# Probabilities as the moving operand: the value product of windowed attention in column tiles, with DVE transposes in place of DMA transposes

## The chip, the cores and the metric

The kernel runs on one core of a Trainium2 chip. The metric is the device time of one execution in microseconds. Names of engines: PE is the tensor engine (PEld its weight loads), ACT the scalar engine, DVE the vector engine, POOL the GpSimd engine, SP the queue that issues DMAs.

## The reference

The output is `g * attention(x) + (1 - g) * swiglu(x)` over 2048 rows of 512 numbers. What matters here is the attention: 32 heads of 16 dimensions, and each query sees only the 256 keys that end at itself.

```python
H = 32; Dh = D // H; W = 256
qkv = (x @ wqkv).reshape(B, S, 3, H, Dh)...
scores = einsum("bhqd,bhkd->bhqk", q, k) * Dh ** -0.5
mask = (idx[:, None] - idx[None, :] >= 0) & (idx[:, None] - idx[None, :] < W)
p = softmax(where(mask, scores, -1e9))
o = einsum("bhqk,bhkd->bhqd", p, v)
a = o.transpose(...).reshape(B, S, D) @ wo
```

The other half, `silu(x @ w1) * (x @ w3) @ w2`, is most of the arithmetic, and its matmuls fill the time between the attention's steps.

## The kernel before

Heads are handled eight at a time (`c`), queries in pairs of 128-row tiles (`p`). A *score burst* makes scores, keys in the partitions, for the eight heads: four matmuls (or eight) in four row tiles of the array at once (strips of 32 of its rows, each with operands of its own). One ACT instruction takes the exponential of all of it, 128x2048, out of a single buffer `big` of four banks of PSUM, the memory that matmuls write to. POOL zeroes what the mask forbids.

```python
# score burst, exponential
big = ps.tile([P, 4, 512], F32, name="big")          # one buffer
for u in range(4):
    nc.tensor.matmul(big[:, u, k * 256:k * 256 + 2 * w],
                     lhsT=kt[32 * u:32 * u + 32, kb * P:(kb + 1) * P],
                     rhs=qz[32 * u:32 * u + 32, :, q0:q0 + w], start=True, stop=True)
nc.scalar.activation(out=e[:, :, 0:2 * n], in_=tl["big"][:, :, 0:2 * n], func=ACT.Exp, scale=SCALE)
```

A *value block* multiplies probabilities by V. The kernel before makes the 128x128 probabilities the stationary operand, so that 17 columns (16 of V and a column of ones, which sums the denominator) stream past it. The result has queries in the partitions; DVE divides it by the denominator, and a DMA turns it into the layout that the output projection needs.

```python
for h8 in range(8):
    ...                                              # two or three key blocks
    nc.tensor.matmul(pva[:, k, h8, :], lhsT=lhsT,    # lhsT: 128x128 probabilities
                     rhs=Vaug[:, kp, 8 * c + h8, :], # 17 columns
                     start=(bi == 0), stop=(bi == len(blocks) - 1))
...
nc.vector.reciprocal(out=st["rden"][:], in_=st["pva"][:, :, :, DH:DH + 1])
nc.vector.tensor_tensor(out=ocur[:], in0=st["pva"][:, :, :, 0:DH],
                        in1=st["rden"][:].to_broadcast([P, 2, 8, DH]), op=ALU.mult)
...
nc.sync.dma_start_transpose(out=OT[:, o:o + P], in_=...ocur...)
```

All instructions are put in order beforehand by a list scheduler in the kernel's own Python text. It knows a duration for each step, slots for the buffers (four PSUM banks `g` for everything but scores), and a due time for each burst (one every 2.55 us). The order on each engine is fixed by it; the hardware only waits.

Names in the lines below: `kt` keys, `qz` masked copies of the queries, `edm` and `ef` probabilities (key blocks on the diagonal and those further back), `tt`, `h` and `hT` the steps of the other half, `OT` the attention's output turned, `ot` a piece of the result. Lines shown are picked out of a view; "..." marks a cut within a sequence in time.

The softmax here doesn't subtract the row's maximum and nothing guards it: scores larger than these inputs give would overflow.

## Time and profile before

| | before |
|---|---|
| median of the first four runs | 257.91 us (257.75 to 258.07) |
| PE / ACT / DVE / POOL busy | 98 / 76 / 59 / 59 % |
| score bursts | 92, one every 2.57 us |
| value blocks | 28 of 48 matmuls, 4 of 24 |

The first lines are from the page of the profile: busy time, share and instructions of each engine, and then the chain of work that ended last, by engine and by line.

```profile
PE 250.7 (98%) x2755; PEld 124.1 (48%) x2755; DVE 151.0 (59%) x267; ACT 195.0 (76%) x143; POOL 150.0 (59%) x251
PE 94%; DMA 2%; SPq 1%; DVE 1%; issue 0%; DVEq 0%
PE g L361 32%; PE g L414 15%; PE g L556 14%; PE big L493 12%; PE g L255 11%; PE g L301 6%; PE g L443 5%; DMA wq_sb<-in_A_wqkv_dram 2%; DMA out_dram<-ot 1%; SPq L571 1%; DVE ot L450 0%; PE g L213 0%; SPq L106 0%; DVE Vaug L311 0%; SPq L453 0%
```

PE is busy 98% of the span and is 94% of the chain, so what shortens PE's work shortens the kernel, until something else becomes the chain. Line 556 is the value matmul and has 14% of the chain. A busy PE alone would not prove this, as the ends of matmuls are modelled in the trace; the chain does.

The next lines are groups of instructions by form: line, engine, operation, operands, count, then busy us and the mean ns of one, then idle time before them and who ended it.

```profile
L501 ACT ACTIVATE edm<-big 128x2048 bf16<-128x2048 f32 x60 | 112.6, 1877 | 29.1 <-PE big L493 16.3 <-POOL edm L510 8.0 <-POOL ef L515 4.6
L556 PE MATMUL g<-Vaug,edm 128*128 128x17 bf16 x992 | 41.5, 171 | 0.0
L562 DVE RECIPROCAL rden<-g 128x16 f32<-128x16 f32 x32 | 8.1, 255 | 12.6 <-PE g L556 12.3
L564 DVE TENSOR_TENSOR ocur<-g,rden 128x256 bf16<-128x256 f32 x32 | 13.6, 425 | 1.1
L510 POOL TENSOR_SCALAR_AFFINE_SELECT edm<-edm 128x512 bf16<-128x512 bf16 x128 | 78.6, 637 | 55.8 <-ACT edm L501 54.3
```

The exponential takes 1.88 us. The value matmuls' 171 ns each are latencies and overlap; their real rate is seen in the chain in order of time (start, us, what):

```profile
102.82 0.33 PE big L493 x8
103.15 0.97 PE g L361 x4
104.12 1.20 PE g L556 x48
105.32 0.23 PE g L361
```

A block of 48 value matmuls takes 1.20 us, 25 ns for each pair of weight load and matmul, and a score burst takes 0.33 us. The matmuls of 512 columns (line 361) take 0.216 us each: 1.73 us for eight. Four of them take 0.97 us where they follow a burst, 0.1 us more than their 0.86: I take this for the change of array mode at the burst, and call it a drain below. The old value block pays none: the matmul after it takes 0.23 us.

The last lines, from the timeline of instructions, show the loop through the single score buffer:

```profile
100.16 0.39 PE L493 MATMUL big<-qz,kt 32*128 32x512 bf16 x4
...
100.67 1.88 ACT L501 ACTIVATE edm<-big 128x2048 bf16<-128x2048 f32 x1 [0.72 <-POOL edm L510]
...
102.75 0.40 PE L493 MATMUL big<-qz,kt 32*128 32x256 bf16 x8
...
103.35 1.87 ACT L501 ACTIVATE ef<-big 128x2048 bf16<-128x2048 f32 x1
```

The exponential starts 0.51 us after this burst begins and ends at 102.55. The next burst begins 0.20 us later, and its exponential after another 0.60 us, one tanh being between. Over all bursts I measured 0.45 us from burst to exponential for bursts of eight matmuls and 0.51 for bursts of four, and from exponential to next burst at least 0.07 us. A turn of this loop thus costs at least about 2.38 us after a burst of eight matmuls and 2.44 after one of four. PE had 2.57 us of work for each turn: the loop was hidden, but only just.

### The profile page before, as it was taken

How to read it: one execution, taken by the hardware profiler on the slowest of the kernel's cores; microseconds unless marked ns; L12 is line 12 of the kernel's file. 1: busy time of each engine (PE TensorE's matmuls, PEld its weight loads, DVE VectorE, ACT ScalarE, POOL GpSimd, SP SyncE). 2: the span in 40 equal slices, each digit the busy share in tenths (PEclk: the TensorE clock that was granted, in tenths of full speed). 3: DMA queues.
4: the chain of work that ended last, by engine and by line, in shares of the span. 5: the costliest groups of instructions: out<-in, count | busy, mean ns of one | idle time of the engine just before them, and what ended most of it. 6: DMA issues, size and time to landing. Idle time of an engine off the chain costs nothing.

```text
span 256.1 us, 6562 instructions
## 1 busy us (share of the span) xinstructions
PE 250.7 (98%) x2755; PEld 124.1 (48%) x2755; DVE 151.0 (59%) x267; ACT 195.0 (76%) x143; POOL 150.0 (59%) x251
## 2 busy tenths in 40 slices
PE   7999999999999999999999999999999999999994
PEld 3545554555545445454555455544563555445552
DVE  2766758766576378456557465637465666454453
ACT  4788788778878888787979797888787878786700
POOL 4275757575565575754755757546737565566610
PEclk9999999999999999999999999999999999999999
DMA  6999921000000000000000000000001111101112
GB/s 196 349 227 286 230 67 13 13 10 8 9 21 3 10 13 11 13 0 13 12 13 14 11 8 5 14 10 13 12 13 13 51 49 47 50 13 50 32 32 87
DMA packets 27014, 13.05 MB, mean 51 GB/s; under 512 B 18309, under 2 KB 26981, under 8 KB 26985
## 3 DMA queue, kind: packets, MB, share of 16 engines
q1 hardware_dynamic: 26424, 12.51, 19.7%
q8 instruction: 21, 0.34, 0.5%
q10 hardware_dynamic: 528, 0.13, 0.2%
q14 instruction: 9, 0.07, 0.1%
q0 software_dynamic: 32, 0.00, 0.0%
HBM read 7.38 MB, written 2.11 MB: 37 GB/s over the span
## 4 chain that ended last, share of the span: by engine, by line
PE 94%; DMA 2%; SPq 1%; DVE 1%; issue 0%; DVEq 0%
PE g L361 32%; PE g L414 15%; PE g L556 14%; PE big L493 12%; PE g L255 11%; PE g L301 6%; PE g L443 5%; DMA wq_sb<-in_A_wqkv_dram 2%; DMA out_dram<-ot 1%; SPq L571 1%; DVE ot L450 0%; PE g L213 0%; SPq L106 0%; DVE Vaug L311 0%; SPq L453 0%
## 5 line engine op out<-in xcount | busy, mean ns | idle before, releaser
L501 ACT ACTIVATE edm<-big 128x2048 bf16<-128x2048 f32 x64 | 116.7, 1824 | 30.4 <-PE big L493 17.5
L510 POOL TENSOR_SCALAR_AFFINE_SELECT edm<-edm 128x512 bf16<-128x512 bf16 x128 | 78.6, 637 | 55.8 <-ACT edm L501 54.3
L515 POOL TENSOR_SCALAR_AFFINE_SELECT ef<-ef 128x512 bf16<-128x512 bf16 x112 | 67.6, 635 | 37.7 <-ACT ef L501 37.7
L361 PE MATMUL g<-xT,w_sb 128*128 128x512 bf16 (+2 forms) x352 | 89.0, 381 | 0.2 <-DVE Vaug L311 0.2
L501 ACT ACTIVATE ef<-big 128x2048 bf16<-128x2048 f32 x28 | 52.5, 1877 | 12.1 <-PE big L493 6.3
L361 PEld LDWEIGHTS <-w_sb 128*128 128x128 bf16 (+2 forms) x352 | 31.4, 100 | 38.2 <-issue 9.0
L378 DVE SCALAR_TENSOR_TENSOR h<-tt,g 128x512 bf16<-128x512 bf16 x40 | 27.4, 686 | 34.5 <-ACT tt L373 34.3
L414 PE MATMUL g<-w_sb,hT 128*128 128x512 bf16 (+1 forms) x176 | 43.1, 380 | 0.0
L556 PE MATMUL g<-Vaug,edm 128*128 128x17 bf16 x992 | 41.5, 171 | 0.0
L556 PEld LDWEIGHTS <-edm 128*128 128x128 bf16 x992 | 38.7, 96 | 4.1
L556 PEld LDWEIGHTS <-ef 128*128 128x128 bf16 x448 | 35.2, 96 | 5.3 <-issue 2.0
L556 PE MATMUL g<-Vaug,ef 128*128 128x17 bf16 x448 | 37.6, 171 | 0.0
L493 PE MATMUL big<-qz,kt 32*128 32x512 bf16 (+1 forms) x480 | 36.0, 329 | 0.0
L384 DVE TENSOR_TENSOR hT<-h,g 128x512 bf16<-128x512 bf16 (+1 forms) x44 | 30.1, 687 | 5.3 <-PE g L361 1.8
L273 DVE TENSOR_SCALAR qz<-g,maskEO 128x512 bf16<-128x512 f32 (+1 forms) x34 | 23.0, 714 | 4.7 <-PE g L255 4.5
L414 PEld LDWEIGHTS <-hT 128*128 128x128 bf16 (+1 forms) x176 | 15.8, 98 | 20.2 <-issue 3.3
L423 DVE TENSOR_SCALAR bsb<-g,omg 128x512 bf16<-128x512 f32 x16 | 12.0, 751 | 22.8 <-PE g L414 22.8
L373 ACT ACTIVATE tt<-g 128x512 bf16<-128x512 f32 x40 | 23.6, 593 | 1.0 <-PE g L361 0.8
L493 PEld LDWEIGHTS <-kt 32*128 32x128 bf16 x480 | 9.8, 92 | 27.9 <-issue 26.6
L255 PE MATMUL g<-xT,wq_sb 128*128 128x512 bf16 (+1 forms) x68 | 17.2, 368 | 0.1
L255 PE MATMUL g<-xT,wk_sb 128*128 128x512 bf16 (+1 forms) x68 | 17.2, 368 | 0.0
L443 PE MATMUL g<-xs,OT 128*128 128x512 bf16 (+1 forms) x68 | 16.0, 367 | 0.0
(38 smaller groups left out, 121.8 us busy)
## 6 DMA issues: line engine op xcount, KB each, us to landing
out_dram<-ot SPq DMA_DIRECT2D x15, 128.0 KB, 1.8
w_sb<-in_B_w_dram SPq DMA_DIRECT2D x2, 864.0 KB, 8.0
w_sb<-in_B_w_dram SPq DMA_DIRECT2D x1, 1280.0 KB, 7.3
xs<-in_A_x_dram SPq DMA_DIRECT2D x4, 256.0 KB, 4.7
w_sb<-in_B_w_dram SPq DMA_DIRECT2D x2, 512.0 KB, 8.2
OT<-ocur SPq DMA_TRANSPOSE x64, 2.3
edm<-in_A_wqkv_dram SPq DMA_DIRECT2D x1, 512.0 KB, 5.4
xs<-in_A_wo_dram SPq DMA_DIRECT2D x2, 256.0 KB, 3.4
```

The lines of the kernel that those rows point to most:

```text
L255: nc.tensor.matmul(b[:, 0:n], lhsT=(wq_sb if is_q else wk_sb)[:, dc, c * P:(c + 1) * P], rhs=xT[:, dc, t0:t1], start=(dc == 0), stop=(dc = ...
L361: nc.tensor.matmul(b[0:m, :], lhsT=wsb[:, dc, f * P:f * P + m], rhs=xT[:, dc, t * 512:(t + 1) * 512], start=(dc == 0), stop=(dc == NDC - 1))
L373: nc.scalar.activation(out=tl["tt"][0:m, :], in_=g_tile[kg][0:m, :], func=ACT.Tanh, scale=0.5)
L378: nc.vector.scalar_tensor_tensor(out=tl["h1"][0:fs, :], in0=tl["tt"][0:fs, :], scalar=1.0, in1=g_tile[kg][0:fs, :], op0=ALU.add, op1=ALU.mult)
L384: nc.vector.tensor_tensor(out=h_tile[t][0:fs, f, :], in0=tl["h1"][0:fs, :], in1=g_tile[ku][0:fs, :], op=ALU.mult)
L414: nc.tensor.matmul(b[:], lhsT=h_tile[t][0:fs, f, (m % 4) * P:(m % 4 + 1) * P], rhs=w2_sb[0:fs, f, :], start=(f == 0), stop=(f == NFC - 1))
L443: nc.tensor.matmul(b[:, 0:n], lhsT=OT[:, c * S + m * P:c * S + (m + 1) * P], rhs=wo_t[c // 2][:, c % 2, n0:n1], start=(c == 0), stop=(c == ...
L493: nc.tensor.matmul(big[:, u, k * 256:k * 256 + 2 * w], lhsT=kt[32 * u:32 * u + 32, kb * P:(kb + 1) * P], rhs=qz[32 * u:32 * u + 32, :, q0: ...
L501: nc.scalar.activation(out=e[:, :, 0:2 * n], in_=tl["big"][:, :, 0:2 * n], func=ACT.Exp, scale=SCALE)
L510: nc.gpsimd.affine_select(out=tri, in_=tri, pattern=[[0, 2], [0, 2], [1, P]], compare_op=ALU.is_ge, fill=0.0, base=0, channel_multiplier=-1)
L515: nc.gpsimd.affine_select(out=tri, in_=tri, pattern=[[0, 4], [-1, P]], compare_op=ALU.is_ge, fill=0.0, base=-1, channel_multiplier=1)
L556: nc.tensor.matmul(pva[:, k, h8, :], lhsT=lhsT, rhs=Vaug[:, kp, 8 * c + h8, :], start=(bi == 0), stop=(bi == len(blocks) - 1))
```

## The change

V becomes stationary: 32 columns of it, 17 useful, in one of four column tiles of the array, and the probabilities stream. A block becomes 40 matmuls of 128 or 256 columns, and its result has head dimensions in the partitions. DVE transposes it in blocks of 32x32 to bring queries into the partitions, divides, and transposes back, straight into the layout that the output projection reads. The 64 DMA transposes fall away. The scheduler learns to put a value block right behind a score burst, so that two changes of array mode become one.

```diff
-    Vaug = pp.tile([P, NT, H, DH + 1], BF16, name="Vaug")
+    Vaug = pp.tile([P, NT, H * (DH + 1) + DH], BF16, name="Vaug")
 ...
-                        nc.tensor.matmul(pva[:, k, h8, :], lhsT=lhsT, rhs=Vaug[:, kp, 8 * c + h8, :], ...)
+            for i in range(2):
+                for bi, (kp, e, cols, (q0, q1)) in enumerate(blocks):
+                    lo, hi = cols(i)
+                    for u in range(4):
+                        h0 = (8 * c + 2 * u + i) * (DH + 1)
+                        nc.tensor.matmul(pva[32 * u:32 * u + 32, i, q0:q1],
+                                         lhsT=Vaug[:, kp, h0:h0 + 32],
+                                         rhs=e[:, u, lo:hi], start=(bi == 0),
+                                         stop=(bi == len(blocks) - 1))
 ...
-                nc.sync.dma_start_transpose(out=OT[:, o:o + P], ...)
+            nc.vector.transpose(out=t1[:], in_=st["pva"].rearrange("p i q -> p (i q)"))
+            ...
+            nc.vector.reciprocal(out=rden[:], in_=t1[:, :, :, DH:DH + 1])
+            nc.vector.tensor_tensor(out=on[:]..., in0=t1[:, :, :, 0:DH],
+                                    in1=rden[:].to_broadcast([P, 2, 8, DH]), op=ALU.mult)
+            nc.vector.transpose(out=OT[:, o:o + 2 * P], in_=on[:].rearrange("p b i d -> p (b i d)"))
 ...
+                    elif o.kind == "pv":
+                        k = -1.5 if last_pe == "burst" or not bursts_left or r_of(o, ro[0]) + 2.6 <= t else 5
```

Left out: the last two down-projection results may be evacuated by ACT, the last two output pieces use other buffers, the warm-up tile shares a buffer, and the ones of `Vaug` are written differently.

More of the change, by code (lines that the diff above doesn't have):

```diff
@@ L51 @@
     xT = pp.tile([P, NDC, S], BF16, name="xT")
-    Vaug = pp.tile([P, NT, H, DH + 1], BF16, name="Vaug")
-    OT = pp.tile([P, NDC * S + P], BF16, name="OT")
+    Vaug = pp.tile([P, NT, H * (DH + 1) + DH], BF16, name="Vaug")
+    OT = pp.tile([P, NDC * S], BF16, name="OT")
     gq = pp.tile([P, NT], F32, name="gq")
@@ L64 @@
     maskEO = pp.tile([P, 2], F32, name="maskEO")
-    warm = pp.tile([P, 512], BF16, name="warm")
     scr = pp.tile([P, 2], F32, name="scr")
@@ L86 @@
     ops = []
-    SLOTS = {"big": 1, "g": 4, "edm": 5, "ef": 3, "hT": 2, "qk": 2, "tt": 2, "h1": 3}
+    SLOTS = {"big": 1, "g": 4, "edm": 5, "ef": 3, "hT": 2, "qk": 2, "tt": 2, "h1": 3, "t1": 1}
     refs = {}
@@ L100 @@
     nc.vector.memset(scr[:], 0.0)
+    warm = sb.tile([P, 512], BF16, name="tt0")
     nc.vector.memset(warm[:], 0.0)
@@ L171 @@
                             op0=ALU.mult, op1=ALU.add)
-    nc.gpsimd.memset(Vaug[:, :, :, DH:DH + 1], 1.0)
+    nc.gpsimd.memset(Vaug[:, :, DH:H * (DH + 1):DH + 1], 1.0)
+    nc.gpsimd.memset(Vaug[:, :, H * (DH + 1):], 1.0)
     class Load:
@@ L291, with v_out @@
     V_op = {}
+    def v_out(m):
+        return Vaug[:, m, 0:H * (DH + 1)].rearrange("p (h d) -> p h d", d=DH + 1)[:, :, 0:DH]
     def add_v(m):
@@ L308, in evac @@
             if eng == "ACT":
-                nc.scalar.copy(out=Vaug[:, m, :, 0:DH], in_=src)
+                nc.scalar.copy(out=v_out(m), in_=src)
             else:
-                nc.vector.tensor_copy(out=Vaug[:, m, :, 0:DH], in_=src)
+                nc.vector.tensor_copy(out=v_out(m), in_=src)
         a0, a = pe_unit(0.87, [pe(i) for i in range(NDC)], [loads["v"]],
@@ L428, in add_down @@
                         up_done[t] + [loads["w2"]], acq=[("g", key)], rel=[("hT", t)], kind="ffn")
-        down_op[m] = Op("DVE", 0.68, evac, [a, gate_op[m // 4]], rel=[("g", key)], rank=0.5)
+        down_op[m] = Op(("ACT", "DVE") if m >= NT - 2 else "DVE", 0.68, evac, [a, gate_op[m // 4]], rel=[("g", key)], rank=0.5)
         return a0
@@ L448, in fin @@
         def fin(eng):
-            ot = smpool.tile([P, D], BF16, name="ot")
+            if n < D:
+                ot = sb.tile([P, 512], BF16, name="h1_0" if n0 else "h1_1")
+            else:
+                ot = smpool.tile([P, D], BF16, name="ot")
             nc.vector.scalar_tensor_tensor(out=ot[:, 0:n], in0=g_tile[key][:, 0:n],
@@ L535, in add_pv @@
         rel.append(("edm", used[1]))
-        def pe(k):
-            def fn():
-                if k == 0:
-                    st["pva"] = bank(key)[:, 0:16 * (DH + 1)].rearrange(
-                        "p (q h d) -> p q h d", q=2, d=DH + 1)
-                pva = st["pva"]
-                qb = 2 * p + k
-                for h8 in range(8):
-                    u, i = h8 // 2, h8 % 2
-                    blocks = []
-                    if qb >= 2:
-                        e = e_tile[("f", c, p - 1)][0]
-                        blocks.append((qb - 2, e[:, u, k * 256 + i * P:k * 256 + (i + 1) * P]))
-                    if qb >= 1:
-                        e, n = e_tile[("d", c, qb - 1)]
-                        blocks.append((qb - 1, e[:, u, i * n + P:i * n + 2 * P]))
-                    e, n = e_tile[("d", c, qb)]
-                    blocks.append((qb, e[:, u, i * n:i * n + P]))
-                    for bi, (kp, lhsT) in enumerate(blocks):
-                        nc.tensor.matmul(pva[:, k, h8, :], lhsT=lhsT, rhs=Vaug[:, kp, 8 * c + h8, :],
-                                         start=(bi == 0), stop=(bi == len(blocks) - 1))
-            return fn
@@ L560, in rec, with pe @@
-        def rec(eng):
-            st["rden"] = smpool.tile([P, 2, 8, 1], F32, name="rden")
-            nc.vector.reciprocal(out=st["rden"][:], in_=st["pva"][:, :, :, DH:DH + 1])
-            ocur = smpool.tile([P, 2, 8, DH], BF16, name="ocur")
-            nc.vector.tensor_tensor(out=ocur[:], in0=st["pva"][:, :, :, 0:DH],
-                                    in1=st["rden"][:].to_broadcast([P, 2, 8, DH]), op=ALU.mult)
-            st["ocur"] = ocur
-        def tr(eng):
-            for k in range(2):
-                o = c * S + (2 * p + k) * P
-                nc.sync.dma_start_transpose(out=OT[:, o:o + P],
-                                            in_=st["ocur"][:, k].rearrange("p h d -> p (h d)"))
+        def pe():
+            pva = bank(key)[:].rearrange("p (i q) -> p i q", i=2)
+            st["pva"] = pva
+            blocks = []
+            e, n = e_tile[("d", c, 2 * p)]
+            blocks.append((2 * p, e, lambda i, n=n: (i * n, i * n + 2 * P), (0, 2 * P)))
+            e, n = e_tile[("d", c, 2 * p + 1)]
+            blocks.append((2 * p + 1, e, lambda i, n=n: (i * n, i * n + P), (P, 2 * P)))
+            if p:
+                e, n = e_tile[("d", c, 2 * p - 1)]
+                blocks.append((2 * p - 1, e, lambda i, n=n: (i * n + P, i * n + 2 * P), (0, P)))
+                e = e_tile[("f", c, p - 1)][0]
+                for k in range(2):
+                    blocks.append((2 * p - 2 + k, e,
+                                   lambda i, k=k: (k * 256 + i * P, k * 256 + (i + 1) * P),
+                                   (k * P, (k + 1) * P)))
+            for i in range(2):
[7 more added lines that the diff above has]
+                                         stop=(bi == len(blocks) - 1))
@@ new lines, in turn, with norm @@
+        def turn(eng):
+            t1 = sb.tile([P, 512], F32, name=f"t1_{slot('t1', key)}")
+            nc.vector.transpose(out=t1[:], in_=st["pva"].rearrange("p i q -> p (i q)"))
+            st["t1"] = t1[:].rearrange("p (i b r) -> p i b r", i=2, r=32)
+        def norm(eng):
+            t1 = st["t1"]
+            rden = sb.tile([P, 2, 8, 1], F32, name="rden")
+            nc.vector.reciprocal(out=rden[:], in_=t1[:, :, :, DH:DH + 1])
+            on = sb.tile([P, 8, 2, DH], BF16, name="on")
+            nc.vector.tensor_tensor(out=on[:].rearrange("p b i d -> p i b d"), in0=t1[:, :, :, 0:DH],
+                                    in1=rden[:].to_broadcast([P, 2, 8, DH]), op=ALU.mult)
+            o = c * S + 2 * p * P
+            nc.vector.transpose(out=OT[:, o:o + 2 * P], in_=on[:].rearrange("p b i d -> p (b i d)"))
@@ L574, in add_pv @@
         deps = [o for u in used for o in e_mask[u]]
         deps += [V_op[m] for m in range(max(0, 2 * p - 2), 2 * p + 2)]
-        a0, a = pe_unit(1.22 if p else 0.6, [pe(0), pe(1)], deps, acq=[("g", key)], rel=rel, kind="pv")
-        b = Op("DVE", 0.6, rec, [a], rel=[("g", key)], rank=-0.6)
-        pv_out[(c, p)] = Op("SP", 2.6, tr, [b])
-        return a0
+        hold("t1", key, 1)
+        a = Op("PE", 0.77 if p else 0.43, pe, deps, acq=[("g", key)], rel=rel, kind="pv")
+        b = Op("DVE", 0.75, turn, [a], rel=[("g", key)], acq=[("t1", key)], rank=-0.6)
@@ L581 @@
+        pv_out[(c, p)] = Op("DVE", 1.3, norm, [b], rel=[("t1", key)], rank=-0.3)
+        return a
     T0, PACE, NWARM = 4.0, 2.55, 7
@@ L670, in next_exp @@
         return free_at["PE"] + 0.65
-    last_kind = None
+    last_pe = None
     strict = True
@@ L696, with r_of @@
             if e == "PE":
+                def r_of(o, r):
+                    return max(ready_time(o, "PE"), 0.0)
                 def pkey(ro):
@@ L722 @@
         o.start, o.eng = t, e
+        if e == "PE":
+            if o.kind == "pv" and last_pe != "burst":
+                o.dur += 0.1
+            last_pe = o.kind
         if e == "SP":
```

## The prediction

> **What bounds the kernel now.** The tensor engine. The page gives PE 98% busy, ACT 76%, DVE 59%, POOL 59%; the chain of waits is 94% PE. Probability-times-value matmuls (line 556) hold 14% of that chain: in the chain in order of time a full block of 48 takes 1.20 us, 25 ns a pair of weight load and matmul, because the 128x128 probabilities are the stationary operand and only 17 columns stream. 28 full and 4 half blocks make 36 us. Close behind: the loop between PE and ACT over the one score buffer: the exponential takes 1.88 us (groups by form), it starts 0.45 to 0.51 us after its score burst, and the next burst has followed an exponential after as little as 0.07 us (timeline). That loop cannot turn faster than about 2.45 us; bursts now come every 2.57 us.
>
> **What changes.** V becomes stationary (32 columns, four column tiles), the probabilities stream. A full block streams 2 x 768 columns per tile, four tiles at once: 40 pairs instead of 48. A 512-column matmul costs 0.216 us in the chain, so 1536 columns are 0.65 us, and a score burst pays about 0.1 us of drain beyond its 0.22 us of streaming on each side: I estimate 0.77 us after a burst (one drain shared; the new order has 28 of 32 blocks there), 0.87 elsewhere, 0.43 for half blocks. The column tiles must run at once. The Trainium skill (TensorEngine Tiling (Array Packing), Key Properties) says tiles load weights and multiply in parallel, and a mode change drains the engine; the trace agrees for row tiles: a burst of four 512-column matmuls lasts 0.39 us. Column tiles no run shows yet. PE saves 28 x 0.43 + 4 x 0.1, about 12.3 us.
>
> DVE gains work: reciprocal and product now cost 0.26 + 0.43 us per block; the new (transpose of 128x512 from PSUM, reciprocal, product, transpose of 128x256) I estimate at 0.75 + 0.25 + 0.42 + 0.4 = 1.8 us, from operations of those sizes. DVE: 151 -> about 187 us (75%). The new product has two SBUF inputs; the Trainium skill (SBUF — State Buffer, Who interferes with whom) says such an operation contends with GpSimd reads; no run here shows it yet. The 64 DMA transposes, off the chain until the tail, vanish.
>
> **How much is on the critical path.** Nearly all of PE's saving is, but the ACT loop takes part back. Summing the new PE order between bursts with these durations, some ten intervals fall to 1.3 to 2.4 us, below what exponential and tanh (1.88 + 0.59 us) allow. Holding each interval at that floor gives back 4 us (0.8 before). Net 8.3 us. The end: the last block's DVE steps, about 2 us, are almost hidden by 8 output matmuls (1.7 us): +0.5 us.
>
> 257.9 - 8.3 + 0.5 is about 250. I predict **249.8 us, range 246.5 to 253.5**; faster by over 2%: 0.83, within 2%: 0.15, slower: 0.02.
>
> **What would show it.** Right: a block takes 0.7 to 0.8 us in the chain, line's share 8 to 10%; PE busy near 240 us, ACT 195 and over 78% of the span; waits of bursts for the exponential appear; DVE near 187. Wrong if: column tiles serialise (blocks near 1.2 us or more: no gain); DVE, busier and blocked by POOL, releases PSUM banks late (waits of PE on DVE); masks come late and blocks wait on POOL.

## The result, and the profile after

| | before | after |
|---|---|---|
| median | 258.16 us (13 runs, 257.75 to 258.46) | 251.48 us (8 runs, 251.21 to 252.08) |
| ratio | | 0.9745 (95%: 0.9735 to 0.9754) |
| PE / ACT / DVE / POOL busy | 98 / 76 / 59 / 59 % | 96 / 78 / 73 / 61 % |
| value block in the chain | 1.20 us | 0.78 us |

The output is correct. The kernel is 6.7 us faster.

The page after: busy times, and the chain by engine and by line (line 565 is the new value matmul, 500 the burst, 508 the exponential, 517 and 522 the masks).

```profile
PE 240.7 (96%) x2499; PEld 104.8 (42%) x2499; DVE 183.0 (73%) x329; ACT 196.4 (78%) x145; POOL 153.2 (61%) x252
PE 84%; ACT 7%; DVE 4%; DMA 2%; issue 1%; POOL 1%; SPq 0%; DVEq 0%; ACTq 0%
PE g L365 28%; PE g L418 16%; PE big L500 12%; PE g L256 9%; PE g L565 9%; PE g L305 6%; ACT edm L508 5%; PE g L447 5%; DMA wq_sb<-in_A_wqkv_dram 2%; ACT ef L508 2%; DVE qz L274 1%; DVE t L572 1%; POOL edm L517 1%; DVE on L580 0%; PE g L214 0%
```

PE lost 10 us of busy time and 10 points of the chain; ACT and DVE, which had next to none, now hold 11% of it. So PE no longer limits everywhere. The groups by form show what was added:

```profile
L565 PE MATMUL g<-edm,Vaug 128*32 128x256 bf16 x256 | 18.0, 278 | 0.0
L572 DVE STREAM_TRANSPOSE t<-g 128x512 f32<-128x512 f32 x32 | 22.8, 714 | 9.5 <-PE g L565 8.9
L578 DVE RECIPROCAL rden<-t 128x16 f32<-128x16 f32 x32 | 8.1, 252 | 1.0
L580 DVE TENSOR_TENSOR on<-t,rden 128x256 bf16<-128x256 f32 x32 | 15.5, 483 | 1.1
L583 DVE STREAM_TRANSPOSE OT<-on 128x256 bf16<-128x256 bf16 x32 | 14.2, 445 | 1.1
L517 POOL TENSOR_SCALAR_AFFINE_SELECT edm<-edm 128x512 bf16<-128x512 bf16 x128 | 81.5, 660 | 52.0 <-ACT edm L508 51.6
```

And in the chain in order of time a value block now looks like this:

```profile
102.96 2.27 PE g L365 x10
105.23 0.33 PE big L500 x4
105.56 0.78 PE g L565 x40
106.33 0.32 PE g L365
```

Forty matmuls take 0.78 us where 48 took 1.20. The line above it is the burst: the block stands directly behind it. The matmul behind the block takes 0.1 us more than its 0.216: the one drain of the two.

Where did PE's time stop being the limit? I compared, between each burst and the next, the time that passed with the PE work that the order puts there. The work is my sum from durations read in the chain: 0.216 us for a matmul of 512 columns and in proportion, 0.43 for a burst with its drains, 0.78 (0.44 for half blocks) for a value block and 0.1 more where it is not behind a burst, 25 ns for an old pair.

| us | first to last burst | PE work in it | PE idle | stretches with over 0.2 idle | last burst to last matmul |
|---|---|---|---|---|---|
| before | 233.8 | 233.0 | 0.7 | 1 (0.4 us) | 10.8 |
| after | 230.3 | 225.3 | 4.9 | 9 (4.5 us) | 7.0 |

Nearly all of the idle time lies in nine stretches between two bursts. Seven of these hold only 1.3 to 2.2 us of PE work, and five of the seven last 2.43 to 2.45 us and one 2.38, whatever their work: 1.29 and 1.73 alike. This is the loop's floor. In seven of the nine, which hold 3.6 of the 4.5 us, the next burst follows the exponential after 0.05 to 0.06 us. One of these seven (at 68.87, 2.75 us) is longer because its exponential started 0.82 us after the burst instead of 0.51; why stays open. The other two wait for something else: one lies at the start, and of its 0.6 us 0.4 were idle before the change too; in the other (at 89.40) PE waited for DVE's product `h`, which had waited for a tanh behind the exponential. The thinnest looks like this in the timeline (brackets: idle before, and who ended it):

```profile
76.14 0.55 DVE L580 TENSOR_TENSOR on<-t,rden 128x256 bf16<-128x256 f32 x1
...
76.82 0.40 PE L500 MATMUL big<-qz,kt 32*128 32x512 bf16 x4
77.10 1.37 DVE L274 TENSOR_SCALAR qz<-g,maskEO 128x512 bf16<-128x512 f32 x2
...
77.15 0.61 PE L365 MATMUL g<-xT,w_sb 128*128 128x512 bf16 x2
77.33 1.88 ACT L508 ACTIVATE edm<-big 128x2048 bf16<-128x2048 f32 x1 [0.24 <-POOL edm L517]
...
78.52 0.59 PE L418 MATMUL g<-w_sb,hT 128*128 128x512 bf16 x2 [0.77 <-DVE qz L274]
...
79.25 0.40 PE L500 MATMUL big<-qz,kt 32*128 32x256 bf16 x8
```

The burst of 76.82 is followed by four matmuls. The second pair had to wait 0.77 us for a PSUM bank: DVE, which held it, was making masked query copies (line 274), and these had queued behind the value block's product and transpose. Then PE reaches the next burst, whose buffer the exponential frees only at 79.21. (The bracket behind the exponential names a mask, as the releaser that came last. The exponential began 0.51 us after its burst, as elsewhere, so the mask did not hold it up.) Two things are late in the same stretch. The waits by engine and line show both, though the totals look small, as a wait is put down to the one releaser that came last:

```profile
PE big L500 <- ACT edm L508: 0.8, 2, 0.6
PE g L418 <- DVE qz L274: 0.8, 1, 0.8
```

### The profile page after: what moved, and what is told of

Same layout as the page of the kernel before. It is cut to its first block, busy times and chain, and to the rows that moved or that the text cites. A ratio compares the mean times of both kernels' runs of the same rounds, so it can differ in the third digit from the quotient of the medians.

```text
span 250.3 us, 5987 instructions
## 1 busy us (share of the span) xinstructions
PE 240.7 (96%) x2499; PEld 104.8 (42%) x2499; DVE 183.0 (73%) x329; ACT 196.4 (78%) x145; POOL 153.2 (61%) x252
## 4 chain that ended last, share of the span: by engine, by line
PE 84%; ACT 7%; DVE 4%; DMA 2%; issue 1%; POOL 1%; SPq 0%; DVEq 0%; ACTq 0%
PE g L365 28%; PE g L418 16%; PE big L500 12%; PE g L256 9%; PE g L565 9%; PE g L305 6%; ACT edm L508 5%; PE g L447 5%; DMA wq_sb<-in_A_wqkv_dram 2%; ACT ef L508 2%; DVE qz L274 1%; DVE t L572 1%; POOL edm L517 1%; DVE on L580 0%; PE g L214 0%
## 5 line engine op out<-in xcount | busy, mean ns | idle before, releaser
L517 POOL TENSOR_SCALAR_AFFINE_SELECT edm<-edm 128x512 bf16<-128x512 bf16 x128 | 81.5, 660 | 52.0 <-ACT edm L508 51.6
L418 PE MATMUL g<-w_sb,hT 128*128 128x512 bf16 (+1 forms) x176 | 43.7, 381 | 1.0 <-DVE qz L274 0.8
L572 DVE STREAM_TRANSPOSE t<-g 128x512 f32<-128x512 f32 x32 | 22.8, 714 | 9.5 <-PE g L565 8.9
L500 PEld LDWEIGHTS <-kt 32*128 32x128 bf16 x480 | 10.4, 92 | 39.9 <-issue 38.7
L565 PEld LDWEIGHTS <-Vaug 128*32 128x32 bf16 x1184 | 20.0, 97 | 8.1 <-issue 6.5
L565 PE MATMUL g<-edm,Vaug 128*32 128x128 bf16 (+1 forms) x736 | 22.7, 240 | 0.0
L427 DVE TENSOR_SCALAR bsb<-g,omg 128x512 bf16<-128x512 f32 x14 | 10.4, 746 | 8.9 <-PE g L418 8.8
L580 DVE TENSOR_TENSOR on<-t,rden 128x256 bf16<-128x256 f32 x32 | 15.5, 483 | 1.1
```

The lines of the kernel that those rows point to most:

```text
L418: nc.tensor.matmul(b[:], lhsT=h_tile[t][0:fs, f, (m % 4) * P:(m % 4 + 1) * P], rhs=w2_sb[0:fs, f, :], start=(f == 0), stop=(f == NFC - 1))
L500: nc.tensor.matmul(big[:, u, k * 256:k * 256 + 2 * w], lhsT=kt[32 * u:32 * u + 32, kb * P:(kb + 1) * P], rhs=qz[32 * u:32 * u + 32, :, q0: ...
L517: nc.gpsimd.affine_select(out=tri, in_=tri, pattern=[[0, 2], [0, 2], [1, P]], compare_op=ALU.is_ge, fill=0.0, base=0, channel_multiplier=-1)
L565: nc.tensor.matmul(pva[32 * u:32 * u + 32, i, q0:q1], lhsT=Vaug[:, kp, h0:h0 + 32], rhs=e[:, u, lo:hi], start=(bi == 0), stop=(bi == len(b ...
L572: nc.vector.transpose(out=t1[:], in_=st["pva"].rearrange("p i q -> p (i q)"))
```

## The experiments

Two theories compete for the 5 us of PE idle time. *Loop theory*: the thin stretches wait for the exponential, since the score loop cannot turn faster than about 2.44 us. *DVE theory*: the busier DVE gives PSUM banks back late. Most experiments keep the changed kernel's order and alter what the hardware does in it. Times are compared by the ratio to the kernel before of the same rounds; one thousandth is 0.26 us. The changed kernel stands at 0.9745.

### Is it the column tiles running at once?

```diff
-                for bi, (kp, e, cols, (q0, q1)) in enumerate(blocks):
-                    lo, hi = cols(i)
-                    for u in range(4):
+                for u in range(4):
+                    for bi, (kp, e, cols, (q0, q1)) in enumerate(blocks):
+                        lo, hi = cols(i)
```

> The changed kernel with the same 40 matmuls of a value block issued column tile by column tile, so that neighbours in the queue use the same tile. If the gain comes from four column tiles running at once, a full block grows from 0.78 us to four times 0.65 us plus drain, about 2.7 us, and the kernel slows by some 28 x 1.9 = 53 us, to about 305 us. If the gain comes from the number of pairs alone (40 instead of 48, same 25 ns each), a block takes about 1.0 us in both orders and the time changes little.

It took 266.23 us (one run, beside 258.36 before) and was correct. The chain in order of time has the block (33 of its 40 matmuls are on the chain):

```profile
101.39 0.33 PE big L500 x4
101.72 1.32 PE g L565 x33
```

A block takes 1.32 us instead of 0.78, and this kernel is slower than the old. So the interleaving over tiles is where the gain comes from; fewer pairs alone would not have done it. But it is not the 2.7 us of one tile after another either. The reason is in PE's timeline, sorted by start:

```profile
101.64 0.41 PE L565 MATMUL g<-edm,Vaug 128*32 128x256 bf16 x4
101.88 0.22 PE L565 MATMUL g<-ef,Vaug 128*32 128x128 bf16 x1
101.89 0.29 PE L565 MATMUL g<-edm,Vaug 128*32 128x128 bf16 x2
101.93 0.22 PE L565 MATMUL g<-ef,Vaug 128*32 128x128 bf16 x1
```

By the program, each tile has three matmuls on `edm` and then two on `ef`. Here four on `edm` (two of 256 and two of 128 columns; the view merges them under the first one's shape) start before the first on `ef`: the 256-column matmul of the next tile starts while three of this tile's are still to come. Here PE itself overlaps neighbouring tiles, about two at a time by the block's time (2.6 / 1.32), even out of program order. Both numbers that I wrote down, 305 us and no change, missed; the direction was that of concurrency.

### What is the scheduler's rule worth?

```diff
-                    elif o.kind == "pv":
+                    elif o.kind == "never":
                         k = -1.5 if last_pe == "burst" or ...
```

> The changed kernel without the scheduler's new rule for value blocks (they are picked by their due time as before, mostly not right after a score burst). My sum of drains says 0.1 us for each of some 26 blocks that lose their place behind a burst: 2.6 us slower, about 254 us, most of it in PE time on the chain. If the score loop between PE and ACT were the only limit, the extra 0.1 us would be absorbed in PE's idle time and the kernel would stay within 1 us of 251.5.

255.72 us, ratio 0.9904: 4.1 us slower than with the rule (0.0159 of 258.3 us), more than the 2.6 written down. In this order 30 blocks instead of 4 do not stand behind a burst. But 13 of the 30 stand directly before one, and these save a drain as well: by starts, 0.31 us pass from the last 512-column matmul to a block or a burst, 0.1 more than its 0.216, and from a block 0.78 us whether a burst or a 512-column matmul follows. That leaves 17 blocks without a neighbouring burst instead of 3, or 1.4 us of drains. From first burst to last matmul the trace shows 4.3 us more (241.6 for 237.3), so some 3 us are idle time of PE. About half of this came after the last burst, where PE waited 0.36 us for a mask within the last block and 1.51 us for the last transpose, against 0.44 us with the rule. So of the 6.7 us, 4.1 hang on the rule, and only about a third of its worth is saved drains. (The order without it was not tuned otherwise, so this is what the rule is worth in this scheduler.)

The opposite part, the rule in the kernel before:

> The kernel before with only the scheduler's new rule (value blocks right behind a score burst) and its old value matmuls. The old matmuls use the full array as their neighbours do, so a place behind a burst spares no drain: I expect no gain, within 1 us of 258.2 us, perhaps slower because a rule tuned for another block length moves work. If the rule itself were what gained, this would show several us less.

259.76 us, ratio 1.0061: 1.6 us slower. The rule gains nothing without the column tiles, as expected; the loss is a little more than the 1 us written down.

### More DVE work

```diff
+            if (c, p) != (NDC - 1, NP - 1):
+                nc.vector.transpose(out=OT[:, o:o + 2 * P], in_=on[:]...)      # again
+                nc.vector.reciprocal(out=rden[:], in_=t1[:, :, :, DH:DH + 1])  # again
```

> The changed kernel with the last transpose and the reciprocal of each value block done twice (but for the last block), the order unchanged: +0.45 + 0.25 us in 31 blocks, 21.7 us more DVE work, about 205 us. If the busier DVE is what ate the missing part of the gain, by giving PSUM banks back late, the time rises by a good share of that, 5 us or more. If the score loop between PE and ACT ate it, DVE still has room (about 45 us) and the time rises by less than 2 us.

255.22 us, ratio 0.9884, so 3.6 us slower; the DVE's busy time rose by 15.8 us (21.7 expected), to 198.8 (79%). That lies between what the two theories said. DVE's share of the chain rose from 4% to 17% (page, chain by engine):

```profile
PE 72%; DVE 17%; issue 4%; ACT 3%; DMA 2%; SPq 1%; DVEq 0%; ACTq 0%
```

PE's idle time between bursts rose from 4.9 to 8.8 us. DVE is close behind the limit, if it is not the limit.

### A longer loop, and three attempts at shorter waits

```diff
-            nc.scalar.activation(out=e[:, :, 0:2 * n], in_=tl["big"][:, :, 0:2 * n], func=ACT.Exp, scale=SCALE)
+            for u0 in (0, 2):
+                nc.scalar.activation(out=e[:, u0:u0 + 2, 0:2 * n], in_=tl["big"][:, u0:u0 + 2, 0:2 * n],
+                                     func=ACT.Exp, scale=SCALE)
```

> The changed kernel with each exponential done as two halves: 2 x 1.02 us instead of 1.88, so the score loop is 0.17 us longer. Holding every interval between bursts at the larger of its PE work and the longer loop, my sum grows by 9.4 us: about 261 us. If the loop has slack and DVE limits, under 2 us slower.

251.84 us, ratio 0.9752: 0.2 us slower, within noise. The lever was far weaker than expected, as the timeline shows:

```profile
102.99 0.40 PE L500 MATMUL big<-qz,kt 32*128 32x256 bf16 x8
...
103.50 1.94 ACT L509 ACTIVATE ef<-big 128x1024 bf16<-128x1024 f32 x2 [0.66 <-PE big L500]
```

The two halves end 1.94 us after the first began, so the loop grew by 0.06 us, not 0.17. I had overlooked what the Trainium skill (ScalarE: Activation LUTs, What ACT_TABLE_LOAD costs) states, that activations back to back overlap by about 93 ns; this trace agrees, with 2 x 1.02 - 1.94 = 0.10 us. The thin stretches that had lasted 2.44 us lasted 2.50 (same table as above, PE idle 5.2 us). That agrees with the loop theory, but it is too small a step to decide by time.

```diff
-                for u in range(4):
-                    nc.tensor.matmul(big[:, u, k * 256:k * 256 + 2 * w], ...)
+                for h in range(2 if w == 256 else 1):
+                    for u in range(4): ...           # 256 columns each
```

> The changed kernel with each four-matmul score burst (512 columns, 64 of 92 bursts) cut into eight matmuls of 256, as the other 28 bursts are. In the traces the exponential starts 0.507 us after a 512-column burst and 0.449 us after a 256-column one, though both take PE 0.33 us of the chain. If the score loop between PE and ACT limits the thin stretches, the loop gets 0.06 us shorter where it binds (some 10 to 20 stretches): 0.6 to 1.2 us faster. If DVE limits, no change (under 0.3 us).

251.75 us, ratio 0.9746: no change, but the edit had not done what it was for. The exponential still started 0.508 us after such a burst (median). The width of the matmuls is not what makes the 0.06 us; what does stays open. This run tells the theories apart no further.

```diff
+                if eng == "DVE":
+                    if i == 0:
+                        nc.vector.tensor_tensor(out=qz[:, :, t0:t1],
+                            in0=g_tile[key][:, 0:n].unsqueeze(1).to_broadcast([P, 2, n]),
+                            in1=maskEO[:].unsqueeze(2).to_broadcast([P, 2, n]), op=ALU.mult)
+                    return
```

> The changed kernel with the two masked copies of each query tile made by one DVE product with broadcast operands (1024 columns) instead of two products of 512 columns: I estimate 1.07 + 0.2 us instead of 2 x 0.735, so about 3 to 4 us less DVE work in 17 places, and the PSUM bank comes back 0.2 us sooner there, the order unchanged. If late banks behind DVE make the thin stretches, 0.5 to 1.5 us faster; by the slope of the run with more DVE work (3.6 us for 15.8 us) about 0.8 us. If the score loop alone limits, no change (under 0.3 us).

251.47 us, ratio 0.9732 (95%: 0.9717 to 0.9748): 0.3 us faster at best and within noise. The table of stretches did not move (idle 4.8 us): where the bank came sooner, the exponential was still awaited.

### Each limit taken away, and both

These runs give wrong results; the order of the other instructions is the same. In the first, ACT reads three of the four head groups, and POOL fills the fourth with ones:

```diff
-            nc.scalar.activation(out=e[:, :, 0:2 * n], in_=tl["big"][:, :, 0:2 * n], ...)
+            nc.scalar.activation(out=e[:, 0:3, 0:2 * n], in_=tl["big"][:, 0:3, 0:2 * n], ...)
 ...
+                if j == (1 if kind == "d" else 3):
+                    nc.gpsimd.memset(e[:, 3, 0:2 * n], 1.0)
+                    if kind == "f":
+                        return
```

> The changed kernel with a wrong result on purpose: the exponential reads only three of the four head groups (GpSimd fills the fourth with ones in place of its mask), about 1.45 us instead of 1.88, so the score loop is 0.4 us shorter, everything else and the order unchanged. If the loop is what the thin stretches of PE work wait for, their idle time shrinks by what my table of intervals gives, 2.9 us: about 248.6 us. If PSUM banks held behind DVE are right behind it, PE waits for DVE there instead and the time stays within 0.7 us of 251.5.

249.63 us, ratio 0.9670: 1.9 us faster than the changed kernel, between the two figures written down. (The filling adds to POOL's work, 179.7 us instead of 153.2.) In the second, the reciprocal and the product of the value block are gone:

```diff
-            nc.vector.reciprocal(out=rden[:], ...)
-            nc.vector.tensor_tensor(out=on[:]..., op=ALU.mult)
-            nc.vector.transpose(out=OT[:, o:o + 2 * P], in_=on[:]...)
+            nc.vector.transpose(out=OT[:, o:o + 2 * P], in_=Vaug[:, 2 * p, 0:2 * P])
```

> The changed kernel with a wrong result on purpose: the reciprocal and the product of each value block are left out, and the last transpose reads a slice of V instead: 0.25 + 0.48 us less in 32 blocks, 23 us less DVE work (about 160 us), the order unchanged. If DVE holds PSUM banks, 2 to 5 us faster. If the score loop limits the thin stretches, the exponential's waits stay and the time falls by under 1 us.

251.38 us, ratio 0.9731: 0.4 us faster. And both:

> Both of the last two at once (wrong result on purpose). If each limit hides the other, this gains clearly more than the two apart together: some 4 to 5 us, down to the PE's own sum, about 246.5 us. If one of them alone limits, it equals that one's run.

248.41 us, ratio 0.9613: 3.4 us faster, more than 1.9 + 0.4. In time alone this surplus of 1.1 us hardly exceeds the intervals of the ratios (0.4 to 0.65 us either way); the traces decide.

| us | first to last burst | PE work in it | PE idle | stretches with over 0.2 idle | last burst to last matmul |
|---|---|---|---|---|---|
| after | 230.3 | 225.3 | 4.9 | 9 (4.5 us) | 7.0 |
| more DVE work | 234.1 | 225.3 | 8.8 | 13 (8.2 us) | 7.0 |
| shorter exponential | 228.3 | 225.3 | 3.0 | 5 (2.5 us) | 7.0 |
| less DVE work | 230.3 | 225.3 | 5.0 | 9 (4.5 us) | 6.4 |
| both | 227.6 | 225.3 | 2.2 | 4 (1.9 us) | 6.4 |

This decides it. Less DVE work alone changes no stretch: its nine stretches are the changed kernel's to within 0.01 us, and all of its 0.4 us is the shorter end, 0.6 us by the trace. A shorter exponential does change them. The exponential lost 0.43 us. The stretch at 41.84 became 0.43 us shorter with it alone; those at 76.82 and 134.99 only 0.33, but 0.43 with both; that at 173.31 even 0.13 longer, but 0.27 shorter with both. The same thin stretch as above, in the chain in order of time, is the exponential's in the run with less DVE work:

```profile
73.66 1.89 ACT edm L508
...
75.61 0.65 POOL edm L517
...
76.27 1.89 ACT edm L508
...
78.20 0.40 PE big L500 x8
```

The mask in it holds up nothing: this exponential, too, began 0.51 us after its burst. In the run with the shorter exponential the stretch is DVE's (line 569 is the value matmul there; then come the block's first transpose, its other DVE steps to the second transpose, the query copies, and the matmuls that needed the bank):

```profile
74.26 0.47 PE g L569 x16
...
74.76 0.73 DVE t L576
...
76.26 0.45 DVE OT L587
76.70 1.30 DVE qz L274 x2
...
78.05 0.59 PE g L418 x2
78.64 0.33 PE big L500 x8
```

So the exponential, by the loop above all, is the first limit: 0.43 us off it are worth about 1.9 us. DVE is the second, right behind it, and hides part of what a faster loop would give. With both eased, the page gives PE the same share of the chain as before the change:

```profile
PE 94%; ACT 2%; DVE 1%; issue 0%; DVEq 0%; ACTq 0%
```

### A better order

My reading of the scheduler, which no run tests by itself, is that the stretches are thin because it found nothing to put there: in its plan PSUM banks were held, or the next burst was thought impossible for 2.51 us. I gave it the measured loop and let the bank-holding DVE work go first:

```diff
-        b = Op("ACT", 1.78 if n == 256 else 1.0, ex, ...)
+        b = Op("ACT", 1.71 if n == 256 else 1.0, ex, ...)
-        pv_out[(c, p)] = Op("DVE", 1.3, norm, [b], rel=[("t1", key)], rank=-0.3)
+        pv_out[(c, p)] = Op("DVE", 1.3, norm, [b], rel=[("t1", key)], rank=0.3)
-    T0, PACE, NWARM = 4.0, 2.55, 7
+    T0, PACE, NWARM = 4.0, 2.45, 7
```

> The changed kernel with three numbers of its scheduler changed: exponential 1.71 us instead of 1.78 (which makes its score loop 2.44 us, as measured, instead of 2.51), bursts due every 2.45 us instead of 2.55, and the product-and-transpose step of a value block ranked behind DVE work that holds PSUM banks. If the thin stretches of PE work are a fault of the order, it fills some of them: 1 to 2 us faster, about 250 us. If they come from the hardware's loop alone, no change.

250.38 us, ratio 0.9698 (95%: 0.9681 to 0.9714), correct: 1.2 us faster than the changed kernel, and the best correct kernel. PE idle time between bursts fell from 4.9 to 2.7 us, in four stretches instead of nine. But the end got worse: after the last burst PE waited 0.36 us for a mask within the last block and 1.28 us for the last transpose, where it had waited 0.44 us. Which of the three numbers does it was not separated.

> A candidate for the best correct kernel: the three scheduler numbers of the earlier rescheduling run with the single masking product. The two are small and aim at the same thin stretches: 0 to 0.5 us better than the rescheduling alone, about 250.1 us, ratio 0.968 to the kernel before.

250.76 us, ratio 0.9705 (95%: 0.9681 to 0.9728): no better than the order alone.

## Why the prediction was right

It said 249.8 us with a range of 246.5 to 253.5; the median is 251.48. Point by point:

- **A value block takes 0.77 us behind a burst.** Measured 0.78. PE's saving over the whole order is then 12.0 us instead of 12.3. The run with one tile at a time shows that it rests on tiles running at once.
- **The score loop takes some 4 us back.** PE's idle time between bursts went from 0.7 to 4.9 us: 4.2 us. The runs with a shorter exponential and with less DVE work show that the exponential is what binds first. The step was right, and so was its size, but partly by luck: the text took its floor from exponential and tanh, 2.47 us of ACT's time. What binds in six of the nine stretches is the turn through the score buffer, 2.44 us after a burst of four and 2.38 after one of eight, which the text names elsewhere. The two floors happen to be nearly equal.
- **The end costs 0.5 us more.** PE waited about 0.4 us for the last transpose, and from the start of the last matmul to the end of the span the trace has about 0.5 us more than before, which I had not counted and did not follow further. The sum of the text was 250.1 us, 1.4 below the result. The end is 0.4 us of this, the blocks 0.3, the loop 0.2, and the kernel before has a median over all 13 runs that is 0.25 above that of the first four, from which the text started; 0.2 to 0.3 us stay unassigned.
- **DVE goes to 187 us.** Measured 183. The transposes took 0.71 and 0.45 us (0.75 and 0.4 expected), reciprocal 0.25, product 0.48 instead of 0.42.
- **DVE stalls would be a reason to be wrong.** They were there, but hidden behind the loop. What I had not seen is that the same stretches carry both, so that mending DVE alone brings little, and mending the exponential alone less than it could.
- **Blocks waiting for masks would be another.** No value block of the changed kernel waited: PE has no idle time before or within any of the 32 in the trace.
- **The share of the chain and waits.** Line 565 has 9% (8 to 10 foretold), ACT is busy 196.4 us and 78%, PE 240.7.

The sum from the traces: from the first burst to the start of the last matmul, 244.5 us became 237.3, 7.2 less; the end gives 0.5 back; 6.7 us remain, as the medians say. (The profiled run's first burst came 1.0 us later than before, but over the profiles of kernels with the same order it came between 7.4 and 9.1 us, so this is the start's scatter, not the change.)

## What to carry to other kernels

When the moving side of a matmul is much narrower than the stationary side (17 columns against 128 here), it is worth trying to swap them and to use column tiles. Interleave the tiles in program order: here the same 40 matmuls took 0.78 us interleaved and 1.32 us tile by tile, more than the 1.20 of the old form. Before counting a saving on the limiting engine, compare each stretch of it with the next slower loop; here idle time took back 4.2 of 12 us, most of it at the loop's floor, where the order left thin stretches. And if easing one suspect changes nothing, ease both before acquitting it: two limits in the same stretch hide each other.

## What the Trainium skill lacked or had wrong

- *TensorE: Matmul & The Clock Gate*, Part 3 (The mechanism), says that matmuls are strictly in order in start and end. Starts were not so in column tiles: with one tile's five matmuls after another's, the next tile's first one started ahead of three earlier ones (0.125 us after the tile before instead of 0.32 us), and a block took 1.32 us where serial tiles would need 8 x 0.32 = 2.6 us by an estimate from 0.216 us for 512 columns.
- *TensorEngine Tiling (Array Packing)*, Key Properties, says that tiles work in parallel and that a change of mode drains the engine; both agree with the trace, but no cost is given. Here a burst with 0.22 us of streaming takes 0.33 us of the chain and about 0.1 us more from its neighbour; a value block and a burst side by side, in either order, pay that 0.1 us once. Four column tiles took 0.78 us for what is 2.6 us of streaming one after another.
- *SBUF — State Buffer*, Who interferes with whom, is right that a DVE instruction with two SBUF inputs contends with a GpSimd one that reads SBUF, and gives no size for this pair. The product with two SBUF inputs took 424 to 835 ns; with one input in PSUM, in the kernel before, 424 to 426 ns. POOL masks that overlapped it took 703 ns on average, the others 635. Whichever came second was delayed by what was left of the first, less 0.14 us (the mask) or 0.15 us (the product), and hardly at all where less than that was left.
- *VectorE: DVE Perf Modes*, The three transpose paths, has one DVE figure, 311 ns for 128x128 bf16. Measured here: 445 ns for 128x256 bf16 within SBUF, 714 ns for 128x512 f32 from PSUM.
